# Attention and expert kernel on one core: one PSUM tile throughout, early expert blocks spread over the last pairs, gathers issued ahead of stores, pair 1's input turns placed between pair 0's scores

## The chip, the cores and the metric

The kernel runs on one core of a Trainium2 chip. The core has four engines that work side by side, each through its own instructions in order: TensorE (PE in the profile; its weight loads are shown apart as PEld), VectorE (DVE), ScalarE (ACT) and GpSimd (POOL). SyncE (SP) issues most DMAs; POOL issues the indirect ones (gathers and scatters by a list of row numbers). PE writes its results into PSUM, which has eight banks of 128 partitions by 512 floats; DVE and ACT read them from there ("evacuate" them) into SBUF, the working memory. POOL does not touch PSUM in this kernel. Engines wait for one another by semaphores.

The metric is the time of one execution on the device in microseconds, as the median of several runs. The profile is of one more execution.

## The reference

```python
def _attn_ref(q, k, v):                      # q, k, v: 8 x 8 x 576 x 64
    scores = scale * np.matmul(q, k.transpose(0, 1, 3, 2))
    mask = block_i >= block_j                # causal by blocks of 64
    scores = np.where(mask, scores, -1000000000.0)
    scores = scores - np.max(scores, axis=-1, keepdims=True)
    attn = np.exp(scores)
    attn = attn / (np.sum(attn, axis=-1, keepdims=True) + 1e-09)
    return np.matmul(attn, v)

def _moe_ref(x, w_gate, w1, w2, capacity):   # x: 8 x 576 x 512, capacity 128
    scores = np.einsum('bsd,d->bs', x, w_gate)
    out = x.copy()
    for b in range(B):
        top_idx = np.argpartition(-scores[b], capacity)[:capacity]
        xe = x[b, top_idx]
        h = np.maximum(xe @ w1, 0.0)         # 512 -> 1024
        ye = h @ w2                          # 1024 -> 512
        g = 1.0 / (1.0 + np.exp(-scores[b, top_idx]))
        out[b, top_idx] = x[b, top_idx] + g[:, None] * ye
```

`x` is the attention's output with its heads side by side. So all rows are written once, and the 128 best rows of each batch are read back, sent through the expert and written again.

## The kernel before, in words

**Attention** runs over 32 pairs of heads (4 for each of 8 batches). For a pair p the steps are: `load` and `load_v` (DMAs on SP); `turn_in` (ten transposes on PE for k, ten for q, which write two PSUM banks) and `keep_in` (two evacuations each, on ACT); `scores` (44 matmuls, in three parts called 2, 1 and 0, into the five score areas of `SETS`); `maxima` (nine row maxima on DVE) and `exps` (nine exponentials on ACT that also sum up); `turn_p` and `keep_p` (transposes of the exponentials on PE and their evacuations on ACT and DVE); `times_v` (the product with v); `denom` (on POOL), `keep_x` (DVE), `turn_x` (PE), `invert` and `divide` (DVE). The last pair of a batch also stores the batch's rows and starts `select`.

The order of instructions on every engine is a list written out by hand: `STEPS` gives each step a due time in units of a pair, the plan holds each step at p + its due time, and the loop emits the first step of the sorted plan that may run (`ready`). Five pairs are thus in flight. `BANK` says which of the eight banks a step takes; `take` and `give` keep account of it. In the kernel before, every pair's `turn_in` takes banks 6 and 7, which are also those of the pair's largest score area (`('s', 0)`).

**Selection.** For each batch `select` makes a chain of small steps: `score` (dot products with `w_gate` on DVE, lines 547 to 552), `flip`, `store` and `fetch` through DRAM or `spread` through PE (lines 575 to 585), `tied` and `once` (ties), `below` (five comparisons of all scores with all, on POOL, for the last batch on DVE), `rank` (six matmuls with ones on PE), `spot` and `find` (DVE, lines 622 to 645), after which the batch's row numbers lie in `idx_all`. Ticks in the plan fit these steps in between attention's; what is left over at the end of attention goes to the expert phase. There `compared` is what remains of batch 5, `older` of batch 6, `last` of batch 7.

**Expert phase.** Batches 0 to 3 are group 0, batches 4 to 7 group 1, 128 rows of each. `gather` (line 890) reads the rows back by an indirect DMA on POOL. `turn_parts` (line 901) transposes them: four PE transposes, a high half on ACT and a low half on DVE, since each operand is split in two numbers that are multiplied as three products. `hidden_parts` (line 934) makes one of eight blocks of the hidden layer for a whole group: 12 matmuls of 512 columns, a Relu on ACT (line 944) and the low half on DVE (line 945). `final` (line 954) makes one batch's output: 24 matmuls, with `between()` called in their middle, which turns the next group's rows, and one DVE instruction for y (line 966), whose buffers number two. `store` (line 970) writes the rows back by an indirect DMA on POOL. All indirect DMAs read or write `out_dram`, so a gather and a store wait for one another's landing.

`halves`, `split1` and `split2` make the two numbers of each weight. For `split2` of even blocks ACT makes the high half and DVE the low one; for odd blocks POOL makes both (lines 865 and 866).

Some expert work stands among the last pairs: the plan goes on for pairs 32 to 36, which do not exist, and `stand_in` uses their turns for the transposes of group 0 (`warm`, four of them) and their scores for three hidden blocks (`fill`, three of them). The kernel before lets one absent pair take as many blocks as there are free single-bank areas. Attention's PSUM tile `ps_all` belongs to a pool that ends with attention; the expert phase opens a second pool, `psum2`, over the same banks.

## Time and profile before

| | |
|---|---|
| median of 3 runs | 426.69 us (426.08 to 426.8) |
| profiled execution | 425.77 us, of which 424.1 us is the span from the first to the last instruction |
| mean granted clock of TensorE | 0.976 |
| busy: PE, PEld, DVE, ACT, POOL | 383.7, 276.1, 312.6, 281.0, 225.5 us |
| DMA | 50.35 MB, 119 GB/s over the span |

Busy times are shares of the whole span, but the stages differ: up to about 290 us attention runs, then its last pairs with early expert work, then the expert phase. So the views by stage, the chain of waits and the order of time say more than the sums. A matmul's end is modelled, so a busy PE is not PE at its peak. The granted clock is the share of TensorE's clock that was passed on.

### The profile page before, as it was taken

The page shows a single profiled execution, that of the slowest core. Times are in us where ns is not written, and L with a number is a line of the kernel's source. Part 1 is how long each engine was busy: PE and PEld are TensorE (multiplying, and loading weights), DVE is VectorE, ACT ScalarE, POOL GpSimd, SP SyncE. Part 2 cuts the span into 40 slices and gives each one's busy share as a digit, 9 for nine tenths or more (in the row PEclk, how much of TensorE's full clock was granted, in tenths as well). Part 3 has the DMA queues.
Part 4 walks back from the last instruction along what each step waited for, and adds up shares of the span by engine and source line. Part 5 has one row for each costly group of instructions (what it writes and reads, how often), then busy time and mean ns, then how long its engine had stood idle before and what let it go on. Part 6 is the DMA issues. An engine that isn't in the chain of part 4 may idle for free.

```text
span 424.1 us, 14177 instructions
## 1 busy us (share of the span) xinstructions
PE 383.7 (90%) x5482; PEld 276.1 (65%) x5482; DVE 312.6 (74%) x704; ACT 281.0 (66%) x969; POOL 225.5 (53%) x370
## 2 busy tenths in 40 slices
PE   3779999999999999998999999998979988299995
PEld 2455677667765777666776667765747866288883
DVE  2457778997998899999899999989459983422222
ACT  3679999999999999989999989987213210112100
POOL 2110174337885223997974993897939893200022
PEclk9889999999999999999999999999998999599999
DMA  9745554945887958387558647425003101200011
GB/s 174 168 107 138 135 127 112 244 99 104 231 189 185 262 128 188 78 238 169 121 160 178 152 146 164 103 59 175 2 0 114 49 0 48 78 25 0 2 49 49
DMA packets 128368, 50.35 MB, mean 119 GB/s; under 512 B 119695, under 2 KB 119725, under 8 KB 128301
## 3 DMA queue, kind: packets, MB, share of 16 engines
q1 hardware_dynamic: 125836, 44.96, 43.7%
q0 software_dynamic: 1280, 4.20, 3.1%
q8 instruction: 43, 0.70, 0.7%
q10 hardware_dynamic: 1184, 0.30, 0.3%
q14 instruction: 25, 0.20, 0.2%
HBM read 37.88 MB, written 11.55 MB: 117 GB/s over the span
## 4 chain that ended last, share of the span: by engine, by line
PE 43%; DVE 15%; ACT 14%; POOL 9%; issue 5%; DMA 3%; SPq 1%; POOLq 0%; ACTq 0%; DVEq 0%
ACT p_sb L414 13%; PE h_ps L938 8%; PE ps L455 6%; PE ps L395 6%; PE y_ps L961 6%; PE ps L486 5%; PE ps L335 5%; DVE nmax L404 4%; POOL more L608 3%; PE ps L938 2%; DMA xe<-out_dram,idx_all 2%; POOL rinv L515 2%; DVE pt L228 2%; PE ps L494 1%; POOL beats1a L610 1%
## 5 line engine op out<-in xcount | busy, mean ns | idle before, releaser
L414 ACT ACTIVATE p_sb<-ps,nmax 128x192 f32<-128x192 f32 (+8 forms) x288 | 147.2, 538 | 22.2 <-DVE nmax L404 17.3
L404 DVE TENSOR_REDUCE nmax<-ps 128x1 f32<-128x192 f32 (+8 forms) x288 | 118.9, 476 | 15.3 <-PE ps L395 13.3
L395 PE MATMUL ps<-kT,qT 64*64 64x64 f32 (+6 forms) x1408 | 90.9, 400 | 0.5 <-DVE xeTl L912 0.5
L515 POOL TENSOR_SCALAR rinv<-sum 64x4 f32<-64x4 f32 (+2 forms) x192 | 50.1, 261 | 71.3 <-ACT pt L221 38.5
L486 PE MATMUL ps<-pt,v 128*64 128x256 f32 (+3 forms) x512 | 76.0, 439 | 1.0 <-ACT pt L221 1.0
L486 PEld LDWEIGHTS ps<-pt,v 128*64 128x64 f32 x512 | 33.9, 136 | 60.2 <-issue 54.4
L455 PE MATMUL ps<-ident,p_sb 64*128 64x64 f32 x1472 | 65.6, 227 | 1.9 <-ACT p_sb L414 0.9
L221 ACT COPY pt<-ps 128x256 f32<-128x256 f32 (+2 forms) x160 | 61.3, 429 | 2.5 <-PE ps L455 1.7
L414 ACT ACTIVATION_READ_ACCUMULATOR p_sb<-ps,nmax 128x1 f32 x288 | 62.6, 217 | 0.0
L455 PEld LDWEIGHTS ps<-ident,p_sb 64*128 64x128 f32 x1472 | 55.5, 141 | 7.5 <-issue 2.5
L395 PEld LDWEIGHTS ps<-kT,qT 64*64 64x64 f32 x1408 | 51.2, 139 | 13.6 <-issue 6.6
L228 DVE COPY pt<-ps 128x512 f32<-128x512 f32 (+1 forms) x96 | 50.3, 552 | 9.3 <-PE ps L455 5.3
L961 PE MATMUL y_ps<-w,h 128*128 128x512 f32 x192 | 47.2, 403 | 1.0 <-DVE h L945 1.0
L961 PEld LDWEIGHTS y_ps<-w,h 128*128 128x128 f32 x192 | 36.9, 194 | 9.7 <-DVE h L945 1.4
L608 POOL TENSOR_SCALAR more<-sB,sc 64x576 bf16<-64x576 f32 (+4 forms) x35 | 41.0, 1180 | 0.8
L971 POOL DMA_INDIRECT out_dram<-y,idx_all x8 | 8.4, 1051 | 54.6 <-DVE y L966 46.0
L225 POOL TENSOR_SCALAR vz<-v 64x512 f32<-64x512 f32 x32 | 21.0, 657 | 29.3 <-DMA v<-in_v_dram 23.3
L228 DVE COPY xt<-ps 128x576 f32<-128x576 f32 x32 | 24.2, 756 | 16.5 <-PE ps L494 13.3
L938 PE MATMUL h_ps<-xeTh,w 128*128 128x512 f32 x104 | 34.6, 408 | 0.0
L549 DVE CUSTOM_DVE_ANT_0 junk<-x_sb,wg_b 128x512 bf16<-128x512 f32 x40 | 33.5, 837 | 0.2
L528 DVE TENSOR_TENSOR x_sb<-ps,rinv 128x640 f32<-128x640 f32 x32 | 26.4, 825 | 8.3 <-PE ps L335 8.1
L927 ACT ACTIVATE gate<-gate 128x1 f32<-128x1 f32 x8 | 1.6, 203 | 43.1 <-DVE gate L923 43.1
(99 smaller groups left out, 522.9 us busy)
## 6 DMA issues: line engine op xcount, KB each, us to landing
v<-in_v_dram SPq DMA_DIRECT2D x64, 128.0 KB, 3.2
out_dram<-x_sb SPq DMA_DIRECT2D x8, 1024.0 KB, 5.4
ld_q<-in_q_dram SPq DMA_DIRECT2D x32, 160.0 KB, 3.4
ld_k<-in_k_dram SPq DMA_DIRECT2D x31, 160.0 KB, 4.1
ld_q<-in_q_dram SPq DMA_DIRECT2D x32, 128.0 KB, 4.1
w_raw<-in_moe_w_dram SPq DMA_DIRECT2D x16, 256.0 KB, 3.9
ld_k<-in_k_dram SPq DMA_DIRECT2D x31, 128.0 KB, 4.3
vz<-in_v_dram SPq DMA_DIRECT2D x64, 32.0 KB, 2.9
```

Source lines behind the costliest of these rows:

```text
L221: nc.scalar.copy(out=o, in_=i)
L228: nc.vector.tensor_copy(out=o, in_=i)
L395: nc.tensor.matmul(place(p, t)[64 * o:64 * o + 64, c0:c1], s["qT"][r, tokens(t, hh)], s["kT"][r, tokens(k0 // 64, hh, c1 - c0)], start=Tru ...
L404: nc.vector.tensor_reduce(out=s["nmax"][:, c:c + 1], in_=place(p, t), axis=AX.X, op=ALU.max, negate=True)
L414: nc.scalar.activation(out=st[p]["p"][:, first(t):first(t) + ends(t)], in_=place(p, t), func=AF.Exp, bias=st[p]["nmax"][:, c:c + 1], scale ...
L455: nc.tensor.transpose(out=ps[:, a, at], in_=win, identity=ident[r, r])
L486: nc.tensor.matmul(x[64 * hh:64 * hh + 64, at + c:1024], vt[:, n, hh, :], s["pt"][:, pt_row(hh, n):pt_row(hh, n) + 512 - 128 * n], start=( ...
L515: nc.gpsimd.tensor_scalar(out=r[to:to + 64, hh, i:i + n], in0=s[64 * a:64 * a + 64, c:c + n], scalar1=1e-9, scalar2=None, op0=ALU.add,)
L549: nc.vector.tensor_tensor_reduce(out=junk[:, 0:DM], in0=x[:, t, :], in1=wg_b, scale=1.0, scalar=0.0, op0=ALU.mult, op1=ALU.add, accum_out= ...
L608: eng.tensor_scalar(out=o[r, c:c1], in0=row["sB"][r, c:c1], scalar1=sc[r, t:t + 1], scalar2=None, op0=op)
L938: nc.tensor.matmul(ps[:, 0:ncol], w1_hl[f][:, a, c, :], xeT[g][d][:, c, 0:ncol], start=(c == 0 and t == 0), stop=(c == NC1 - 1 and t == 2),)
L961: nc.tensor.matmul(ps[0:n, 0:DM], h_tile(f)[:, a, begin[g][gi]:begin[g][gi] + n], late["w2"][f][:, d, :], start=(f == 0 and t == 0), stop= ...
```

## The change

- `ps_all` is made once for the whole kernel. In the expert phase `open_bank` hands out its banks in turn: 0 to 3 for tag `w`, 4 and 5 for `s`, 6 and 7 for `wide`. `banks["free"]` goes.
- `SECOND` gives pair 1 its own due times: its k turn right behind pair 0's scores 2, its q turn right behind pair 0's scores 0, its own scores 2 earlier. The inputs of pairs 1 and 2 take banks 2 and 3 (`bank`).
- Matmuls of constants: 11 of 512 columns first of all on PE (`wake(WARM)`), and 4 of 128 columns behind each of pair 0's two input turns.
- An absent pair takes at most one hidden block (`filled`), and one more is emitted right behind the last pair's product with v; its evacuation comes after attention's last step.
- In `split2` ACT makes the high halves of all blocks; POOL makes the low half of the odd ones.
- In the expert phase, batch 5's `once` comes first of all, its rank and its spots each one block later, the weight splits ahead of each hidden block. Batch 6's rank, spots and index come in the middle of the third final tile. The stores of group 0 come behind its fourth tile, and y has four buffers.

```diff
+WARM, WAKE = 11, 4
+SECOND = {
+    ('turn_in', 'k'): 1.1192,
+    ('turn_in', 'q'): 1.3146,
...
+    ('scores', 2): 1.9619,
+}
...
+    psum = ctx.enter_context(tc.tile_pool(name="psum", bufs=1, space=PSUM))
+    ps_all = psum.tile([P, 8, 512], F32, name="ps")
...
+        def bank(p, use):
+            return BANK["x"] if p in (1, 2) and use[0] == "in" else BANK[use]
...
-                    plan.append((p + at, i, p, name, args))
+                    plan.append((SECOND.get((name, *args), p + at) if p == 1 else p + at, i, p, name, args))
...
+        def wake(n, cols=4):
+            for _ in range(n):
+                nc.tensor.matmul(spare()[:, 0:cols * P], ones_b, ones_b.unsqueeze(1).to_broadcast([P, cols, P]), start=True, stop=True)
+        wake(WARM)
...
-                    elif name == "scores" and fill and not warm and len(BANK[use]) == 1 and not any(v for u, v in parts.items() if u[0] == "in"):
+                    elif name == "scores" and fill and p not in filled and not warm and len(BANK[use]) == 1 and not any(v for u, v in parts.items() if u[0] == "in"):
+                        filled.add(p)
...
+                if name == "turn_in" and p == 0:
+                    wake(WAKE, 1)
+                if name == "times_v" and p == N - 1 and fill and not warm:
+                    parts["last"] = list(hidden_parts(0, fill.pop(0), spare()))
...
     def split2(f):
         w = late["w2"][f]
-        halves(late["raw"][:, f, :], w[:, 0], w[:, 1], f % 2 == 1)
+        raw = late["raw"][:, f, :]
+        nc.scalar.copy(out=w[:, 0], in_=raw)
+        eng = nc.gpsimd if f % 2 else nc.vector
+        eng.tensor_tensor(out=w[:, 1], in0=raw, in1=w[:, 0].bitcast(F32), op=ALU.subtract)
...
-        y = late["pool"].tile([P, DM], F32, name="y", bufs=2)
+        y = late["pool"].tile([P, DM], F32, name="y", bufs=4)
...
-        psum = ctx.enter_context(tc.tile_pool(name="psum2", bufs=3, space=PSUM))
-        banks["wide"] = lambda name: psum.tile([P, 2, 512], F32, tag="wide", bufs=1, name=name)
+        turns_of = {"w": [0, 1, 2, 3], "s": [4, 5]}
+        def open_bank(tag, name):
+            x = turns_of[tag].pop(0)
+            turns_of[tag].append(x)
+            return ps_all[:, x, :]
+        banks["wide"] = lambda name: ps_all[:, 6:8, :]
...
         for i, f in enumerate(fill + list(range(EARLY, NC2))):
-            hidden(0, f)
+            if i == 0:
+                run(compared, "tied")
             for _ in range(3):
                 if rest:
                     split2(rest.pop(0))
-            if i == 0:
-                run(compared, "tied", "rank")
+            hidden(0, f)
             if i == 1:
+                run(compared, "rank")
+                run(last, "spread")
+            if i == 2:
                 run(compared, "spot", "find")
                 gather_ready(1)
-                run(last, "spread")
-            if i == 2:
                 run(older, "tied", "below")
                 run(last, "tied")
...
-                stores.append(final(g, gi, lambda: turns(nx if gi == n - 1 else 2)))
+                def between():
+                    if gi == 2:
+                        run(older, "rank", "spot", "find")
+                    turns(nx if gi == n - 1 else 2)
+                stores.append(final(g, gi, between))
...
                 if gi == 1:
                     run(last, "spot", "find")
-                    run(older, "rank")
-                if gi == 2:
-                    run(older, "spot", "find")
                 gather_ready(g + 1)
-                if gi or n == 1:
+                if gi == n - 1 or not nx:
                     for store in stores:
                         store()
                     stores = []
```

More of the change, by code (lines that the diff above doesn't have):

```diff
@@ L124 @@
 PRELOAD = {"load": 3, "load_v": 2}
+WARM, WAKE = 11, 4
+SECOND = {
+    ('turn_in', 'k'): 1.1192,
+    ('turn_in', 'q'): 1.3146,
+    ('keep_in', 'k', 0): 1.1782,
+    ('keep_in', 'k', 1): 1.1802,
+    ('keep_in', 'q', 0): 1.5108,
+    ('keep_in', 'q', 1): 1.5128,
+    ('scores', 2): 1.9619,
+}
 ENGINE = {
@@ L236, in attention @@
         sm = att.enter_context(tc.tile_pool(name="sm", bufs=2))
-        psum = att.enter_context(tc.tile_pool(name="psum", bufs=1, space=PSUM))
-        ps_all = psum.tile([P, 8, 512], F32, name="ps")
         pairs = [(b, h) for b in range(B) for h in range(0, H, 2)]
@@ L245, in attention @@
         live = [None] * 8
+        def bank(p, use):
+            return BANK["x"] if p in (1, 2) and use[0] == "in" else BANK[use]
         def take(p, use, reads):
-            for x in BANK[use]:
+            for x in bank(p, use):
                 assert live[x] is None, (p, use, live)
                 live[x] = [p, use, reads]
-            x = BANK[use]
+            x = bank(p, use)
             return ps_all[:, x[0]:x[-1] + 1, :]
         def give(p, use):
-            for x in BANK[use]:
+            for x in bank(p, use):
                 assert live[x][0:2] == [p, use], (p, use, live)
@@ L286, in attention @@
         banks["hold"] = lambda z: (take(z, "rk", 1)[:, 0, :], lambda: give(z, "rk"))
-        banks["free"] = lambda: any(live[x] is None and room(x) > 0.14 for x in range(8))
         def held(n, shape, name, zero, value=0.0):
@@ L764, in ready @@
                 live[x] is None
-                for use in uses.get(name, lambda *x: [])(*args) if firsts[use] == (name, args) for x in BANK[use]
+                for use in uses.get(name, lambda *x: [])(*args) if firsts[use] == (name, args) for x in bank(p, use)
             )
-        parts = {}
+        parts, filled = {}, set()
         def stand_in(p, name, args):
@@ L861, in load_w2 @@
         del w2_rows[:n]
-    def halves(raw, hi, lo, pool_engine=False):
-        if pool_engine:
-            nc.gpsimd.tensor_scalar(out=hi, in0=raw, scalar1=1.0, scalar2=1.0, op0=ALU.mult, op1=ALU.mult)
-            nc.gpsimd.tensor_tensor(out=lo, in0=raw, in1=hi.bitcast(F32), op=ALU.subtract)
-        else:
-            nc.scalar.copy(out=hi, in_=raw)
-            nc.vector.tensor_tensor(out=lo, in0=raw, in1=hi.bitcast(F32), op=ALU.subtract)
     def split1(f):
         w = w1_hl[f]
-        halves(w1_raw[:, :, f * P:(f + 1) * P], w[:, 0], w[:, 1], True)
+        raw = w1_raw[:, :, f * P:(f + 1) * P]
+        nc.gpsimd.tensor_scalar(out=w[:, 0], in0=raw, scalar1=1.0, scalar2=1.0, op0=ALU.mult, op1=ALU.mult)
+        nc.gpsimd.tensor_tensor(out=w[:, 1], in0=raw, in1=w[:, 0].bitcast(F32), op=ALU.subtract)
     def split2(f):
         w = late["w2"][f]
-        halves(late["raw"][:, f, :], w[:, 0], w[:, 1], f % 2 == 1)
+        raw = late["raw"][:, f, :]
+        nc.scalar.copy(out=w[:, 0], in_=raw)
+        eng = nc.gpsimd if f % 2 else nc.vector
+        eng.tensor_tensor(out=w[:, 1], in0=raw, in1=w[:, 0].bitcast(F32), op=ALU.subtract)
     def run(chain, *names, n=None):
@@ L985, in experts @@
     def experts():
-        psum = ctx.enter_context(tc.tile_pool(name="psum2", bufs=3, space=PSUM))
-        banks["wide"] = lambda name: psum.tile([P, 2, 512], F32, tag="wide", bufs=1, name=name)
-        banks["free"] = lambda: True
-        banks["hold"] = lambda z: (banks["open"]("w", "rk_ps"), lambda: None)
-        banks["open"] = lambda tag, name: psum.tile([P, 512], F32, tag=tag, bufs={"w": 4, "s": 2}[tag], name=name)
+        turns_of = {"w": [0, 1, 2, 3], "s": [4, 5]}
[4 more added lines that the diff above has]
+        banks["wide"] = lambda name: ps_all[:, 6:8, :]
+        banks["hold"] = lambda z: (open_bank("w", "rk_ps"), lambda: None)
+        banks["open"] = open_bank
         open_late()
```

## The prediction, made before the changed kernel ran

> **What bounds the kernel now.** I read the page first, then busy time and granted clock by stage, then the chain that ended last, then the order of time at the places where TensorE (PE) stands idle. The page says that no engine but PE is near its span:
>
> ```profile
> span 424.1 us, 14177 instructions
> PE 383.7 (90%) x5482; PEld 276.1 (65%) x5482; DVE 312.6 (74%) x704; ACT 281.0 (66%) x969; POOL 225.5 (53%) x370
> ```
>
> The 10% are not spread evenly. Stretches of my choice, in us (the first five lie between changes of the clock); the columns are the length, the busy time of PE, PEld, DVE, ACT and POOL, PE's granted clock, DMA share and GB/s:
>
> ```profile
> 14.42:17.83 3.41, 0.37 (x6) 0.11 (x4) 1.89 (x3) 2.69 (x11) 0.00 (x0) 1.00 0.98 199
> 17.83:21.24 3.41, 3.41 (x52) 3.19 (x56) 1.29 (x2) 2.03 (x6) 1.97 (x7) 0.50 0.57 126
> 21.24:24.66 3.42, 2.42 (x38) 1.08 (x30) 3.01 (x8) 2.23 (x11) 0.00 (x0) 1.00 0.55 147
> 24.66:28.07 3.41, 1.56 (x43) 1.46 (x45) 0.95 (x4) 3.41 (x13) 0.70 (x3) 1.00 0.01 2
> 28.07:31.48 3.41, 3.41 (x49) 3.01 (x53) 1.50 (x3) 2.47 (x9) 0.69 (x3) 0.50 0.80 176
> 47.40:50.20 2.80, 2.80 (x52) 1.60 (x49) 2.41 (x8) 2.43 (x10) 1.59 (x6) 1.00 0.63 139
> 304.00:318.10 14.10, 11.03 (x88) 7.72 (x86) 6.37 (x15) 2.00 (x4) 7.03 (x12) 1.00 0.01 1
> 318.10:343.00 24.90, 23.81 (x117) 18.64 (x117) 23.94 (x35) 6.44 (x13) 22.89 (x17) 0.93 0.22 70
> 360.47:368.25 7.78, 0.00 (x0) 0.03 (x1) 3.44 (x10) 0.20 (x1) 1.97 (x2) 0.64 0.21 73
> 368.25:374.07 5.82, 5.82 (x21) 4.98 (x21) 1.38 (x2) 1.17 (x2) 0.98 (x1) 0.61 0.12 45
> ```
>
> Three places lose time: the fill of the pipeline (to about 32 us, clock 0.50 twice), the end of attention (3.1 us idle in 304 to 318, then a stage in which DVE is busy 23.94 of 24.90 us), and 7.78 us without a matmul at 360. Between 40 and 290 us nothing is edited. The chain that ended last shows what the end of the kernel waits for (start, length, what):
>
> ```profile
> 302.00 8.62 PE ps L938 x36
> ...
> 344.60 5.54 PE y_ps L961 x24
> ...
> 353.03 5.04 DMA xe<-out_dram,idx_all
> 358.34 2.75 DMA out_dram<-y,idx_all
> 361.21 0.75 DVE y L966
> 361.96 0.86 DVE here L629 x2
> 362.84 0.76 DVE junk L638
> 364.89 3.22 DMA xe<-out_dram,idx_all
> 368.25 1.94 PE xe_ps L909 x8
> 370.19 4.04 PE y_ps L961 x12
> 374.23 22.48 PE h_ps L938 x96
> ```
>
> A gather of batch 7 (353.03), a store (358.34), the index of batch 6 and its gather (364.89) stand in a row in front of the turns at 368.25.
>
> **Part 1, the start.** In order of time (start, length, engine and line; in brackets the idle time before it and what ended it):
>
> ```profile
> 5.75 0.80 PE L335 MATMUL ps<-ident,ld_k 64*128 64x64 f32 x10 [5.75 <-DMA ld_k<-in_k_dram]
> 9.64 5.05 PE L395 MATMUL ps<-kT,qT 64*64 64x64 f32 x44
> 12.24 0.42 ACT L414 ACTIVATE p_sb<-ps,nmax 128x192 f32<-128x192 f32 x1 [1.82 <-DVE nmax L404]
> 17.73 0.75 PE L335 MATMUL ps<-ident,ld_q 64*128 64x64 f32 x10 [3.04 <-ACT p_sb L414]
> 19.61 1.29 DVE L228 COPY pt<-ps 128x512 f32<-128x512 f32 x2 [2.88 <-PE ps L455]
> 22.43 0.42 ACT L414 ACTIVATE p_sb<-ps,nmax 128x192 f32<-128x192 f32 x1 [1.54 <-DVE nmax L404]
> 32.02 0.42 ACT L414 ACTIVATE p_sb<-ps,nmax 128x192 f32<-128x192 f32 x1 [1.48 <-DVE nmax L404]
> 40.78 0.42 ACT L414 ACTIVATE p_sb<-ps,nmax 128x192 f32<-128x192 f32 x1 [0.38 <-DVE nmax L404]
> 47.47 2.71 PE L395 MATMUL ps<-kT,qT 64*64 64x64 f32 x44
> 49.38 0.42 ACT L414 ACTIVATE p_sb<-ps,nmax 128x192 f32<-128x192 f32 x1 [0.37 <-POOL vz L225]
> ```
>
> The first exponentials of pairs 0, 1, 2, 3 and 4 start at 12.24, 22.43, 32.02, 40.78 and 49.38: distances 10.19, 9.59, 8.76 and 8.60, the last being the steady one. Pair 1 is late because its q turn (17.73) needs banks 6 and 7, which pair 0 holds until its exponentials of them are done (PE idle 3.04, ended by ACT). The change gives it banks 2 and 3 and places both turns and the first scores of pair 1 ahead of that. If every distance becomes 8.60, 1.59 + 0.99 + 0.16 = 2.74 us are gained. The first exponentials also come earlier: pair 0's scores are slow (5.05 against 2.71 later), and the distance from scores to exponentials is 2.60 against 1.91 (47.47 to 49.38), so a warm clock gives 0.69; pair 1's k turn no longer lies ahead of these scores, ten transposes at 0.75 (row 17.73), of which I count 0.7, since its two evacuations stay on ACT ahead of the exponentials. Together 4.1. One pair is likely to meet a cold clock still, half of 0.69 off: **3.8 us**. The bounds: if the clock gains nothing and DVE's copies at 19.61 to 20.90, which stay ahead of pair 1's maxima, hold it, at most 22.43 - 20.90 = 1.5 us and perhaps 0.5 is left; above, 4.8 if pair 1 follows pair 0 faster than 8.60, while no older pair competes for ACT.
>
> The 11 warming matmuls have no row. A 512-column matmul goes by in 5.54 / 24 = 0.23 us (344.60); eleven take 2.5 us, or 5.1 at half the clock, and PE waits 5.75 us for its first data: nothing, or up to 0.4 us where they start late. The 4 small ones behind each of pair 0's turns lie in PE's wait for the evacuation: nothing. Pair 2's turns use banks 2 and 3 too, which pair 0's third turn needs next; ACT's evacuation lies between them already: nothing, or 0.75 (ten transposes) if it comes late. Loads keep their order on SP; a load of pair 4 waits for pair 1's turns, which come earlier. Everything after shifts as a whole, for the order is fixed.
>
> Of the clock, the rows say: a stretch with 0.37 of 3.41 us busy and one with 1.56 of 3.41 were each followed by clock 0.50; one with 2.42 of 3.42 was not. [...] I follow the rows; it widens the range upwards.
>
> **Part 2, early blocks and the shared PSUM tile.** The first row is that of line 549 alone between 318 and 325 us, with the shortest, middle and longest of five; the others are of the order of time:
>
> ```profile
> L549 DVE CUSTOM_DVE_ANT_0 junk<-x_sb,wg_b x5: 692/974/1778, 318.1 to 323.3; 128x512 bf16<-128x512 f32 x5
> ...
> 317.22 0.82 DVE L528 TENSOR_TENSOR x_sb<-ps,rinv 128x640 f32<-128x640 f32 x1
> 318.14 1.11 POOL L865 TENSOR_SCALAR w<-w_raw 128x512 fp32r<-128x512 f32 x1 [6.47 <-DVE x_sb L528]
> 318.19 0.80 PE L335 MATMUL sb_ps<-ident,sc 64*128 64x64 f32 x10 [1.48 <-DVE x_sb L528]
> 342.28 0.68 DVE L945 SCALAR_TENSOR_TENSOR h<-h_ps,h 128x512 fp32r<-128x512 f32 x1
> 343.01 0.50 PE L961 MATMUL y_ps<-w,h 128*128 128x512 f32 x1 [1.01 <-DVE h L945]
> 350.05 1.28 POOL L610 TENSOR_TENSOR beats0b<-beats0b,more 128x576 bf16<-128x576 bf16 x1
> ```
>
> Before, three early blocks stand in one piece (8.62) ahead of the last pair's product with v; then PE waits in turn for that pair's evacuations and, for the release of the whole old PSUM tile, for the last division (1.48). After, one block stays there, one follows the product, one lies between the last two turns. PE can win its 3.1 us of idle, and 1.7 for the clock of 0.93 over 24.9 us, 4.8 in all. But the stage behind belongs to DVE, and the last matmul of the first final product waits for DVE's h (343.01). DVE can begin earlier by PE's waits ahead of the last turn, 3.1 - 1.48 = 1.6 us, less the low halves of two blocks at 0.68, one now ahead of the last division and one right behind it: 0.3 to 1.0, I take 0.7. The five scores of the last batch then take about 6 us on DVE (the last begins 5.2 behind the first), while PE has two blocks, 5.6 us, before their spread: a new PE wait of about 1 us, off the path as long as DVE sets the end. Four first passes over odd w2 blocks leave POOL for ACT (1.11 each on POOL, 4.4 in all; ACT is busy 6.44 of 24.90 us there). A score on DVE takes between 0.69 and 1.78, the long ones beside POOL's work, so DVE may get 0 to 3 us back; I take 1.4. Sum **2.1 us**. From below -1.0: the indices of batch 5 come one block later on DVE, its gather and POOL's comparisons of batch 6 queue behind them. From above 4.0. POOL's comparisons then end not at 351.33 but about 2 us earlier.
>
> **Part 3, gathers ahead of stores.** By the chain above, from 353.03 to 374.23, batch 6 is picked only after the third y, which waits for its buffer, that is for the first store, which waits for the gather of batch 7. After, four y buffers exist, stores come behind the fourth tile, and batch 6's rank stands in the middle of the third. Let E be the end of the second final product, 344.60 + 5.54 = 350.1 now. PE then does half a tile (2.8), six rank matmuls (about 0.8), two more halves (5.5) and arrives at the turns at E + 9.1. The index: rank done at E + 3.6, then 0.86 + 0.76 and about 0.8 of hand-overs, gather out at E + 6.0, landed 3.22 to 5.04 later: E + 9.2 to 11.0. PE waits 0.1 to 1.9, I take 0.7, since 3.22 is the gather at the same place: turns at E + 9.8, where they were at 368.25 = E + 18.1. Gain 8.3. Without the idle stretch the clock holds: 12 matmuls take 2.8 for 4.04, and the eight turns 1.94 x 0.61 = 1.2: 2.0 less. Sum **10.3 us**, bounds 5.5 (POOL late by 3 us, slow gather) and 11.0. The four stores now run one after the other, 4 x 2.75 = 11 us on POOL's queue, behind 22.5 us of hidden blocks; without that cover the next y would wait for them. `banks["free"]` is read nowhere: nothing.
>
> **Sum.** 3.8 + 2.1 + 10.3 = 16.2. The profiled execution took 425.77 (span and 1.67 around it), so 409.6; the median of the runs, 426.69, lies 0.92 higher: **410.5 us**. Lower bounds together give 5.0, or 421.7; upper ones 19.8, or 406.9.
>
> **Rivals.** (a) POOL or the gather holds PE: rank 6 now sits ahead of half a tile in PE's queue and waits for the chain that ended at 351.33; if DVE and PE come 2.1 us earlier and POOL does not, or the gather is a 5.04, PE waits 2 to 4 us more: about 413. For it: POOL is busy 22.89 of 24.90; against: it loses 4.4 us. (b) The start's gain doesn't arrive, since DVE's copies hold pair 1 or the clock stays cold, so the warming doesn't do what it says: 3.3 less, 413.8. For it: the clock was 0.50 twice after short idle; against: no queue waits there for a load. (c) Slower: one tile for all banks is tracked as a whole, so that PE's next block waits until ACT and DVE have read the last one. Each of 13 hidden blocks would expose about 1.3 us (0.68 on DVE and nearly as much on ACT), 8 final tiles 0.75 each: 17 + 6 = 23, some 433; it decides once 16.2 / 1.3 = 13 blocks expose it. Against: 47.40 to 50.20, where PE is busy 2.80 of 2.80 on this same tile beside DVE's 2.41 and ACT's 2.43.
>
> **How the numbers follow.** Forecast (407 to 413) 0.62, (a) 0.16, (b) 0.13, (a) and (b) together (up to 421) 0.06, (c) and the like 0.02, no change 0.01. Holding 8 in 10 takes 406.5 to 416.0. Faster by over 0.2% (about what a measurement of this kernel can tell) 0.96, within 0.01, slower 0.03.
>
> **What would show it.** Right: exponentials of pair 3 near 37 us; no PE wait for the last division, yet PE waiting for DVE's h near 336; both late gathers ahead of all stores and PE idle under 2 us before the last turns, clock 1.00 there; the hidden blocks of group 1 starting near 358. Wrong: pair 3 at 39 or later, rank 6 waiting for POOL, or PE idle above 3 us at the turns.

## The result, and the profile after

The changed kernel takes 411.9 us (median of four executions, 410.73 to 412.17) against 426.75 for the kernel before beside it: a ratio of 0.9642, 95% interval 0.9611 to 0.9674. The forecast was 410.5. The profiled execution took 411.95 us, 410.2 of it the span. Two executions of the experiments below, one of 539.39 us (e2) and one of 2033.32 us (e6), were disturbed and are left out of their medians.

The busy times of its page, and a stretch of 270 us (columns as in the prediction):

```profile
PE 383.2 (93%) x5501; PEld 271.9 (66%) x5501; DVE 313.1 (76%) x704; ACT 282.4 (69%) x973; POOL 219.6 (54%) x366
...
10.00:280.00 270.00, 257.80 (x4734) 179.01 (x4730) 237.75 (x550) 249.43 (x892) 156.84 (x287) 1.00 0.65 157
```

Between 10 and 280 us the granted clock is full. No engine has much less to do; the span shrank around the same work. To see where, I cut every span at three events: **A** runs from the start to the first exponential of pair 31, **B** to the last division of attention, **C** to the first matmul of group 1's hidden blocks, and **D** is the rest. Before, the two outer events are these (the division, 317.22, stands in the prediction):

```profile
286.34 0.42 ACT L414 ACTIVATE p_sb<-ps,nmax 128x192 f32<-128x192 f32 x1 [0.94 <-DVE nmax L404]
...
374.07 0.40 PE L938 MATMUL h_ps<-xeTh,w 128*128 128x512 f32 x1
```

After, in order of time (the first five exponentials are those of pairs 0 to 4; in brackets the idle time ahead and what ended it):

```profile
10.83 0.44 ACT L428 ACTIVATE p_sb<-ps,nmax 128x192 f32<-128x192 f32 x1
19.00 0.42 ACT L428 ACTIVATE p_sb<-ps,nmax 128x192 f32<-128x192 f32 x1 [0.86 <-DVE nmax L418]
27.20 0.42 ACT L428 ACTIVATE p_sb<-ps,nmax 128x192 f32<-128x192 f32 x1 [0.29 <-PE ps L409]
36.13 0.42 ACT L428 ACTIVATE p_sb<-ps,nmax 128x192 f32<-128x192 f32 x1 [0.79 <-DVE nmax L418]
44.51 0.42 ACT L428 ACTIVATE p_sb<-ps,nmax 128x192 f32<-128x192 f32 x1 [0.34 <-POOL vz L235]
...
281.38 0.42 ACT L428 ACTIVATE p_sb<-ps,nmax 128x192 f32<-128x192 f32 x1 [0.94 <-DVE nmax L418]
...
290.73 4.04 PE L500 MATMUL ps<-pt,v 128*64 128x512 f32 x16 [0.96 <-ACT pt L231]
...
313.04 0.82 DVE L542 TENSOR_TENSOR x_sb<-ps,rinv 128x640 f32<-128x640 f32 x1
...
338.64 0.50 PE L984 MATMUL ps<-w,h 128*128 128x512 f32 x1 [2.38 <-DVE h L968]
...
350.21 1.24 POOL L918 DMA_INDIRECT xe<-out_dram,idx_all  x1 [4.01 <-DVE idx_all L655]
353.27 0.96 POOL L918 DMA_INDIRECT xe<-out_dram,idx_all  x1 [1.82 <-DVE idx_all L655]
...
356.58 1.07 PE L932 MATMUL ps<-ident,xe 128*128 128x128 f32 x8 [0.18 <-DMA xe<-out_dram,idx_all]
...
357.26 1.00 POOL L994 DMA_INDIRECT out_dram<-y,idx_all  x1 [3.04 <-DMA xe<-out_dram,idx_all]
...
360.24 0.40 PE L961 MATMUL ps<-xeTh,w 128*128 128x512 f32 x1
```

So A went from 286.34 to 281.38, B from 30.88 to 31.66, C from 56.85 to 47.20, and D stayed at 50.0. The whole gain of 13.8 us between the two spans lies in A (4.96) and C (9.65); B lost 0.78. Both late gathers now go out ahead of the first store (357.26), and the wait of 7.79 us ahead of the last turns is 0.18.

The busy time by stretches of the changed kernel shows two stretches at half the clock (second and fourth row), each behind one in which PE waited (first and third row). The fifth row is the stage that DVE keeps busy, the last the way to the turns, where the long wait stood before:

```profile
287.87:291.28 3.41, 1.80 (x24) 1.20 (x24) 3.41 (x9) 2.26 (x8) 2.78 (x8) 1.00 0.09 20
291.28:294.69 3.41, 3.41 (x20) 1.65 (x18) 0.70 (x1) 0.00 (x0) 3.23 (x3) 0.50 0.00 0
335.65:339.07 3.42, 1.03 (x5) 0.45 (x4) 3.42 (x6) 0.00 (x0) 3.24 (x4) 1.00 0.00 0
339.07:342.48 3.41, 3.01 (x11) 2.00 (x11) 2.98 (x8) 1.17 (x3) 3.41 (x3) 0.50 0.00 0
...
313.04:338.64 25.60, 22.16 (x107) 16.99 (x108) 25.07 (x37) 8.19 (x16) 17.46 (x14) 1.00 0.20 68
347.32:356.58 9.26, 9.08 (x43) 6.88 (x42) 6.89 (x20) 0.41 (x2) 2.19 (x2) 1.00 0.19 58
```

Between 313 and 339 DVE is busy 25.07 of 25.60 us. The chain that ended last says what it does there (start, length, what):

```profile
333.33 1.18 DVE beats1a L618
334.55 0.69 DVE h L968
335.24 1.94 DVE beats1a L618 x2
...
337.98 0.60 DVE h L968
...
341.15 6.17 PE ps L984 x24
...
353.27 3.17 DMA xe<-out_dram,idx_all
```

PE's last matmul of the first final product needs the h made at 337.98, and that one stands in DVE's queue behind comparisons of batch 7 which nobody needs yet.

### The profile page after: what moved, and what is told of

Read it like the earlier page. It is cut to its first block, busy times and chain, and to the rows that moved or that the text cites. A ratio compares the mean times of both kernels' runs of the same rounds, so it can differ in the third digit from the quotient of the medians.

```text
span 410.2 us, 14213 instructions
## 1 busy us (share of the span) xinstructions
PE 383.2 (93%) x5501; PEld 271.9 (66%) x5501; DVE 313.1 (76%) x704; ACT 282.4 (69%) x973; POOL 219.6 (54%) x366
## 4 chain that ended last, share of the span: by engine, by line
PE 43%; ACT 17%; DVE 14%; POOL 10%; issue 5%; DMA 1%; POOLq 0%; SPq 0%; ACTq 0%; DVEq 0%
ACT p_sb L428 15%; PE ps L961 8%; PE ps L469 7%; PE ps L984 6%; PE ps L409 6%; PE ps L500 6%; PE ps L349 6%; POOL more L622 3%; DVE nmax L418 3%; POOL rinv L529 2%; DVE junk L563 2%; DVE pt L238 2%; PE ps L508 2%; POOL beats1a L624 1%; DVE junk L652 1%
## 5 line engine op out<-in xcount | busy, mean ns | idle before, releaser
L409 PE MATMUL ps<-kT,qT 64*64 64x64 f32 (+6 forms) x1408 | 88.8, 387 | 1.2 <-ACT qT L233 0.5
L500 PE MATMUL ps<-pt,v 128*64 128x256 f32 (+3 forms) x512 | 77.6, 446 | 1.0 <-ACT pt L231 1.0
L409 PEld LDWEIGHTS ps<-kT,qT 64*64 64x64 f32 x1408 | 49.2, 133 | 14.5 <-issue 5.7
L984 PE MATMUL ps<-w,h 128*128 128x512 f32 x192 | 46.8, 400 | 2.4 <-DVE h L968 2.4
L984 PEld LDWEIGHTS ps<-w,h 128*128 128x128 f32 x192 | 36.4, 191 | 11.2 <-DVE h L968 3.2
L961 PE MATMUL ps<-xeTh,w 128*128 128x512 f32 x128 | 41.8, 400 | 0.7 <-DVE h L968 0.7
L967 ACT ACTIVATE h<-ps 128x512 fp32r<-128x512 f32 x16 | 9.5, 598 | 38.6 <-PE ps L961 38.6
L563 DVE CUSTOM_DVE_ANT_0 junk<-x_sb,wg_b 128x512 bf16<-128x512 f32 x40 | 33.6, 839 | 0.1
```

The source lines that it names most:

```text
L409: nc.tensor.matmul(place(p, t)[64 * o:64 * o + 64, c0:c1], s["qT"][r, tokens(t, hh)], s["kT"][r, tokens(k0 // 64, hh, c1 - c0)], start=Tru ...
L500: nc.tensor.matmul(x[64 * hh:64 * hh + 64, at + c:1024], vt[:, n, hh, :], s["pt"][:, pt_row(hh, n):pt_row(hh, n) + 512 - 128 * n], start=( ...
L563: nc.vector.tensor_tensor_reduce(out=junk[:, 0:DM], in0=x[:, t, :], in1=wg_b, scale=1.0, scalar=0.0, op0=ALU.mult, op1=ALU.add, accum_out= ...
L961: nc.tensor.matmul(ps[:, 0:ncol], w1_hl[f][:, a, c, :], xeT[g][d][:, c, 0:ncol], start=(c == 0 and t == 0), stop=(c == NC1 - 1 and t == 2),)
L984: nc.tensor.matmul(ps[0:n, 0:DM], h_tile(f)[:, a, begin[g][gi]:begin[g][gi] + n], late["w2"][f][:, d, :], start=(f == 0 and t == 0), stop= ...
```

## The experiments

Every edit is against the changed kernel unless another is named. A, B and C are of each kernel's profiled execution.

| kernel | median us | ratio to before (95%) | A | B | C |
|---|---|---|---|---|---|
| before | 426.75 | | 286.34 | 30.88 | 56.85 |
| changed | 411.9 | 0.9642 (0.9611 to 0.9674) | 281.38 | 31.66 | 47.20 |
| e1: no constant products | 414.43 | 0.9728 (0.968 to 0.9776) | 287.56 | 29.98 | 46.98 |
| e2: pair 1 as before | 414.44 | 0.9737 (0.9675 to 0.98) | 283.90 | 31.67 | 47.16 |
| e3: before, gathers first | 415.31 | 0.9763 (0.9708 to 0.9817) | 284.53 | 30.88 | 47.05 |
| e4: early blocks in one piece | 413.74 | 0.9717 (0.9669 to 0.9764) | 281.33 | 30.88 | 48.17 |
| e5: own PSUM pool for experts | 415.1 | 0.9751 (0.9695 to 0.9807) | 283.36 | 29.98 | 49.58 |
| e6: odd high halves on POOL | 412.56 | 0.969 (0.9638 to 0.9742) | 284.68 | 29.99 | 48.21 |
| e7: low halves first | 409.16 | 0.961 (0.9557 to 0.9663) | 281.59 | 31.64 | 43.83 |
| e8: six more constant products | 411.46 | 0.9641 (0.9592 to 0.9691) | 284.75 | 29.99 | 47.83 |
| e9: old order of the early blocks | 416.29 | 0.9798 (0.9756 to 0.984) | 280.79 | 29.99 | 53.11 |
| e10: e7 with 18 constant products | 410.89 | 0.9623 (0.9565 to 0.9681) | 284.99 | 30.00 | 43.84 |
| e11: e10, a gate later | 409.84 | 0.9596 (0.9537 to 0.9654) | 285.39 | 29.98 | 42.79 |
| e12: e11 without 8 of them | 408.04 | 0.9578 (0.9549 to 0.9606) | 283.82 | 30.00 | 42.76 |

(The kernel before ran again beside each group of experiments, with medians from 425.79 to 426.42. The ratios are to these, and of means, not of medians.)

Read the columns before the medians. B takes only three values: 30.88 where all three early blocks stand in one piece, 29.98 to 30.00 with the change's placing, and 31.64 to 31.67 with the same placing where the clock falls ahead of pair 30's product with v (4.04 us at 290.73 above; the same product of pair 31 takes 2.37). A differs by up to 4 us between kernels that are identical up to there: 280.79 to 284.75 over the changed kernel, e4, e5, e6, e7, e8 and e9, 282.55 on average. The start of before, in before and e3, gave 286.34 and 284.53, 285.44 on average.

What differs between those seven is the clock. A is 280.79 to 281.59 in the four profiles that have one stretch of 3.41 us at half the clock in the start, or none (changed, e4, e7, e9), 283.36 in the one with two (e5), and 284.68 and 284.75 in the two with three (e6, e8). These are e8's three, the last two side by side:

```profile
17.31:20.72 3.41, 3.41 (x30) 1.85 (x24) 2.92 (x8) 1.98 (x8) 1.27 (x4) 0.50 1.15 231
24.13:30.96 6.83, 6.07 (x80) 5.04 (x84) 2.59 (x7) 5.04 (x18) 2.00 (x7) 0.50 0.61 146
```

C lies between 46.98 and 47.83 in the changed kernel, e1, e2 and e8, whose code is the same in that stage.

### Undoing one part at a time

**e1**, no constant products:

```diff
-WARM, WAKE = 11, 4
+WARM, WAKE = 0, 0
```

> The changed kernel without its 11 + 8 matmuls of constants. Theory (of the 5.0 us that the start gained, 28 to 49 us, most comes from where pair 1's turns stand and 1 to 2 us from the clock): pair 0's first exponentials near 11.5 to 12 us instead of 10.8, granted clock 0.50 in at least one stretch before 32 us, pair 4's first exponentials at 45.5 to 46.5 instead of 44.5, total 412.9 to 413.9 us. Rival (the warm clock is most of the start's gain): pair 4 at 48 or later, total 415 us or more. Rival (the constants do nothing, PE waits for data there): 411.9 us.

2.5 us slower by the medians, between the theory and the rival. What the products do stands in the last 24 matmuls of pair 0's scores, in e1 and in the changed kernel:

```profile
11.31 3.69 PE L409 MATMUL ps<-kT,qT 64*64 64x448 f32 x24
```

```profile
10.09 1.95 PE L409 MATMUL ps<-kT,qT 64*64 64x448 f32 x24
```

Without the products they take nearly twice as long and end 2.96 us later, at 15.00 for 12.04. In the three profiles without products (before, e1, e3) pair 0's first exponentials start between 12.05 and 12.24 us, in the eleven with them between 10.43 and 11.17. So the products act on the time of the first scores, by my estimate through the clock: 1.9 times as long is near what half the clock cost at the end (4.04 us for pair 30's product with v, 2.37 for pair 31's). No row of the granted clock shows it: for before it reads 1.00 between 9.64 and 14.42, where pair 0's scores take 5.05 us. Nor do the products make sure of the clock behind the first scores: this profile, the slowest execution of e1 (416.23), has 10.2 us at half the clock in the start, but so has e8, which has the products. Pair 4's first exponentials, at 50.67, are on the rival's side (48 or later), but at 48.23 so are e8's. B and C are no worse.

**e2**, pair 1 in its old order and old banks:

```diff
-SECOND = {
-    ('turn_in', 'k'): 1.1192,
...
-}
+SECOND = {}
...
-            return BANK["x"] if p in (1, 2) and use[0] == "in" else BANK[use]
+            return BANK[use]
```

> The changed kernel with pair 1's due times and banks as before, the constants kept. Theory: pair 1's q turn waits again for pair 0's exponentials in banks 6 and 7; exponentials of pairs 0, 1 and 2 about 10 us apart instead of 8.2; pair 4's first exponentials at 47 to 48 us, total 414.5 to 415.5 us. Rival (the warm clock alone gives the gain): 411.9 to 412.9 us.

2.5 us slower by the medians; the two intervals only just part (from 0.9675 here, up to 0.9674 for the changed kernel). In the profile all of it is in A (B and C are the changed kernel's to 0.04), but 283.90 lies among the values that the changed start gave, 280.79 to 284.75, so the profile alone shows nothing. Nor does it show the step of the theory:

```profile
15.24 0.53 PE L341 MATMUL ps<-ident,ld_q 64*128 64x64 f32 x10 [3.19 <-ACT p_sb L420]
...
19.48 0.42 ACT L420 ACTIVATE p_sb<-ps,nmax 128x192 f32<-128x192 f32 x1 [1.52 <-DVE nmax L410]
```

Pair 1's q turn does wait 3.19 us for pair 0's exponentials, as before. Yet its first exponentials come 8.31 us behind pair 0's (11.17), not 10, and pair 4's at 46.85, hardly later than e5's 46.71 with the new order. The medians say that the order of pair 1 is worth something; how stays open.

**e3**, the kernel before with the third part alone (four y buffers, batch 6's rank and index in the third tile, stores behind the fourth):

```diff
-        y = late["pool"].tile([P, DM], F32, name="y", bufs=2)
+        y = late["pool"].tile([P, DM], F32, name="y", bufs=4)
...
+                    if gi == 2:
+                        run(older, "rank", "spot", "find")
...
-                if gi or n == 1:
+                if gi == n - 1 or not nx:
```

> The kernel before with part 3 alone: batch 6's rank, spots and index in the middle of the third final tile, stores of group 0 behind the fourth, four y buffers. Theory: PE's 7.8 us without a matmul shrink to under 2 us and the cold clock behind them goes: 10.3 to 11 us less than before, 415.7 to 416.4 us. Rival (POOL, which still makes the high halves here, holds the rank of batch 6 and with it PE): a gain of 6 to 8 us, 418.5 to 420.5 us, with PE waiting for beats0b at the rank.

With this part alone the time falls by 11.1 us (from 426.42, the median of the kernel before beside it), of the 14.9 of the whole change; this is the theory. Between the profiles the span falls by 11.6: 9.8 in C, from 56.85 to 47.05, and 1.8 in A, whose code is that of before, so that this is scatter. PE's wait ahead of the turns is gone here too:

```profile
358.79 1.06 PE L909 MATMUL xe_ps<-ident,xe 128*128 128x128 f32 x8 [0.23 <-DMA xe<-out_dram,idx_all]
```

With part 3 alone C is 47.05; with everything it is 47.20. **Part 2 as a whole does nothing in C.**

**e4**, the three early blocks in one piece again:

```diff
-                    elif name == "scores" and fill and p not in filled and not warm and ...
+                    elif name == "scores" and fill and not warm and ...
...
-                if name == "times_v" and p == N - 1 and fill and not warm:
-                    parts["last"] = list(hidden_parts(0, fill.pop(0), spare()))
```

> The changed kernel with the three early blocks in one piece again ahead of the last pair's product with v, one PSUM tile kept. Theory (the spread blocks free the last pair's evacuations, but DVE sets the end of the stage): DVE begins the scores of batch 7 about 0.5 to 1.5 us later, total 412.4 to 413.4 us. Rival (PE sets the stage, two blocks of 2.9 us moved behind the product are won in full): 414.5 us or more. Rival (it is worth nothing or costs): 411.9 us or less.

1.8 us slower by the medians, between the theory and the rival; the intervals overlap a little. B is 30.88, which is 0.9 worse than the change's placing at the full clock, and C is 48.17, 0.3 to 1.2 worse than the 46.98 to 47.83 above. The changed kernel's own profile gained nothing from the placing in B only because its clock fell there.

**e5**, a PSUM pool for the experts alone:

```diff
-    psum = ctx.enter_context(tc.tile_pool(name="psum", bufs=1, space=PSUM))
-    ps_all = psum.tile([P, 8, 512], F32, name="ps")
...
+        psum = att.enter_context(tc.tile_pool(name="psum", bufs=1, space=PSUM))
+        ps_all = psum.tile([P, 8, 512], F32, name="ps")
...
-        banks["open"] = open_bank
+        psum = ctx.enter_context(tc.tile_pool(name="psum2", bufs=3, space=PSUM))
...
+        banks["open"] = lambda tag, name: psum.tile([P, 512], F32, tag=tag, bufs={"w": 4, "s": 2}[tag], name=name)
```

> The changed kernel with a PSUM pool of its own for the experts, as before, so that the first product of the experts' stage waits for the last division of attention. Theory: DVE sets the end of this stage and PE's wait (1.48 us before) lies beside it: 411.9 to 412.9. Rival: PE's wait is paid in full, with the cold clock that an idle PE meets: 413.5 to 415.

3.2 us slower, C 2.4 longer: the rival. In order of time, and the clock behind it:

```profile
314.91 0.79 PE L348 MATMUL sb_ps<-ident,sc 64*128 64x64 f32 x10 [2.70 <-DVE h L967]
```

```profile
314.65:318.06 3.41, 3.15 (x16) 2.58 (x17) 3.27 (x10) 2.27 (x5) 0.41 (x1) 0.50 0.90 319
```

PE waits 2.70 us for DVE's h, which reads the old tile, and behind that the clock falls. That DVE is busy all the time did not make PE's wait free.

**e6**, the first pass over odd w2 blocks back on POOL:

```diff
-        nc.scalar.copy(out=w[:, 0], in_=raw)
+        if f % 2:
+            nc.gpsimd.tensor_scalar(out=w[:, 0], in0=raw, scalar1=1.0, scalar2=1.0, op0=ALU.mult, op1=ALU.mult)
+        else:
+            nc.scalar.copy(out=w[:, 0], in_=raw)
```

> The changed kernel with the first pass over odd w2 blocks (128x512, 1.11 us each, four of them) back on POOL. Theory: POOL's passes make DVE's scores long (0.69 to 1.78 us) and DVE sets the end of the stage: 0.5 to 1.5 us slower, 412.4 to 413.4. Rival: POOL has slack there and DVE's scores are long either way: 411.4 to 412.2; or POOL's comparisons of batch 6 end 4.4 us later and PE waits for them: 414 or more.

0.7 us slower by the medians, within the scatter; C is 48.21, 0.4 to 1.2 longer than the 46.98 to 47.83 above. The reason I gave for it is half right. The groups by line with their shapes (count, busy us, mean ns) give DVE's five scores of batch 7 (L549 or L563), before, after and in e6, and the low halves that DVE makes:

```profile
L549 DVE CUSTOM_DVE_ANT_0 junk<-x_sb,wg_b 128x512 bf16<-128x512 f32 x5 | 6.1, 1213 | 0.2
```

```profile
L563 DVE CUSTOM_DVE_ANT_0 junk<-x_sb,wg_b 128x512 bf16<-128x512 f32 x5 | 6.3, 1263 | 0.1
...
L900 DVE TENSOR_TENSOR w<-w_raw,w 128x512 fp32r<-128x512 f32 x4 | 3.1, 806 | 0.0
```

```profile
L563 DVE CUSTOM_DVE_ANT_0 junk<-x_sb,wg_b 128x512 bf16<-128x512 f32 x5 | 6.0, 1199 | 0.1
...
L903 DVE TENSOR_TENSOR w<-w_raw,w 128x512 fp32r<-128x512 f32 x4 | 4.6, 1176 | 0.0
```

The scores cost about the same three times. What e6 lengthens is DVE's own low halves, from 3.1 to 4.6 us. POOL's passes do make the scores long, though, in each of these kernels, and the low halves in the same way. Three rows of the changed kernel show how:

```profile
314.38 0.68 DVE L563 CUSTOM_DVE_ANT_0 junk<-x_sb,wg_b 128x512 bf16<-128x512 f32 x1
...
314.72 1.49 POOL L900 TENSOR_TENSOR w<-w_raw,w 128x512 fp32r<-128x512 f32 x1 [6.32 <-ACT w L898]
...
315.11 1.65 DVE L563 CUSTOM_DVE_ANT_0 junk<-x_sb,wg_b 128x512 bf16<-128x512 f32 x1
```

The score that starts ahead of POOL's pass takes 0.68 us. The next one starts inside the pass and ends 0.55 us behind its end (316.21). All fourteen profiles agree: of these scores and low halves between 310 and 345 us, the 58 that start inside one of POOL's passes over a weight end 0.53 to 0.55 us behind that pass, and the 61 that start while POOL is idle take 0.67 to 0.69 us. In the changed kernel three of the five scores and one of DVE's four low halves start inside such a pass; in e6, where POOL has more passes, all five scores, some of them near the pass's end, and three of the low halves.

**e9**, the old order in the loop over the early blocks:

```diff
         for i, f in enumerate(fill + list(range(EARLY, NC2))):
-            if i == 0:
-                run(compared, "tied")
+            hidden(0, f)
             for _ in range(3):
                 if rest:
                     split2(rest.pop(0))
-            hidden(0, f)
+            if i == 0:
+                run(compared, "tied", "rank")
...
```

> The changed kernel with the order of steps in the loop over the three early blocks as before (hidden block ahead of the comparisons of batch 6, rank 6 and spread 7 where they stood), all else changed. Theory: PE waited 1.06 us for the score of batch 7 (320.94) and 2.38 for h (338.64) in the changed kernel, DVE sets the end of this stage, so the order of PE's work does nothing: 411.5 to 412.5. Rival: the new order costs time, since rank 6's index is later on DVE: 409.5 to 411; or it is what hides spread 7: 413 to 414.5.

(The rank in question is batch 5's; the expectation names batch 6 by mistake. The lines left out move batch 5's rank and index ahead by one block, as before.) 4.4 us slower, C 5.9 longer, more than either of the rivals allowed: my theory that this order does nothing fell. In order of time on PE, ACT and POOL:

```profile
318.71 0.28 PE L633 MATMUL ps<-ties,ones_b 128*128 128x288 bf16 x1 [4.78 <-POOL ties L609]
...
313.77 0.60 ACT L967 ACTIVATE h<-ps 128x512 fp32r<-128x512 f32 x1 [2.80 <-PE ps L961]
314.26 1.65 ACT L898 CAST w<-w_raw 128x512 fp32r<-128x512 f32 x3
...
315.47 1.39 POOL L900 TENSOR_TENSOR w<-w_raw,w 128x512 fp32r<-128x512 f32 x1 [8.84 <-ACT w L898]
316.82 1.84 POOL L609 TENSOR_TENSOR ties<-ties,later 128x640 bf16<-128x640 bf16 x1
```

The ties of batch 5 stand on POOL behind the low half of an odd block. That low half now waits 8.84 us for ACT's high half, and ACT makes it (314.26) only behind the Relu of a block (313.77). PE waits 4.78 us at the third matmul of the rank. Moving the high halves to ACT makes POOL's queue hang on ACT's; pulling `tied` to the front of the loop is what pays for it. In e3 the old order stands with POOL making both halves, and C is 47.05. The two edits of part 2 that I costed apart are one.

### What the wait for h costs, and a better version

**e7**, the second half of batch 7's comparisons behind the three blocks, its rank in the middle of the second tile:

```diff
-            if i > 1:
-                run(last, "below", n=2)
+        run(last, "below")
...
+                    if gi == 1:
+                        run(last, "rank")
...
-                    run(last, "spread", "tied", "below", "rank")
+                    run(last, "spread", "tied", "below")
```

> The changed kernel with the order of DVE's work at the end of attention changed: the second comparisons (below) of batch 7 come behind all three early expert blocks instead of two by two between them, so that DVE makes the low halves of f6 and f7 first, and rank 7 is issued in the middle of the second final product. Theory: in the changed kernel PE waits 2.38 us for DVE's h ahead of the last matmul of the first final product (338.64) and runs cold behind it (339.07 to 342.48); with h ready early neither is left, some 2.4 + 0.6 = 3 us, so 408.5 to 409.5 against 411.9. Rival: DVE's work is only moved; rank 7 and then POOL's comparisons of batch 6 come later, PE waits at rank 6 or at the turns: 410.5 to 412.5.

2.7 us faster than the changed kernel by the medians, as the theory had it, though the intervals of the two ratios overlap. C is 3.4 shorter, 43.83 here and 43.84 in e10, which has the same code there. Both low halves are made at once, and the first final product runs through, at the full clock:

```profile
331.23 1.28 DVE L968 SCALAR_TENSOR_TENSOR h<-ps,h 128x512 fp32r<-128x512 f32 x2
...
333.43 5.77 PE L984 MATMUL ps<-w,h 128*128 128x512 f32 x24
...
353.40 1.07 PE L932 MATMUL ps<-ident,xe 128*128 128x128 f32 x8 [1.22 <-DMA xe<-out_dram,idx_all]
```

**e8**, constant products in two more of PE's waits at the end of attention:

```diff
+                if name == "times_v" and p == N - 2:
+                    wake(4)
...
+                if name == "turn_in" and p == N + 1 and args[0] == "k":
+                    wake(2)
```

> The changed kernel with six more warming matmuls (128x512, 0.23 us each at the full clock): four ahead of the product with v of pair 30 (PE was idle 0.96 us there) and two ahead of the stand-in turns behind the last pair (idle 0.65 us). Theory: the clock of 0.50 from 291.28 to 294.69 of the changed kernel goes away and 1.7 us with it; the one behind the wait for h (339.07) stays, so the last division is 30.0 us behind the first exponentials of pair 31 instead of 31.7, and the time is 409.5 to 411.5. Rival: the stage behind takes the gain back, since POOL's comparisons of batch 6 set rank 6 and DVE sets h: 411.5 to 412.5; or the warming matmuls delay the product: 412.5 to 413.

B is 29.99 and the time 411.46 against 411.9, too little to tell. In the four profiles with these products (e8, e10 to e12) the clock never falls in B; in the seven with the same placing and without them it falls in three (changed, e2, e7) and not in four (e1, e5, e6, e9). That the clock loss in B costs 1.68 us is shown; that the products prevent it is not.

**e10** is e7 with e8's six products and twelve more ahead of the first four `turn_p`:

```diff
-        parts, filled = {}, set()
+        parts, filled, idle_turns = {}, set(), [4, 3, 2, 3]
...
+                if name == "turn_p" and idle_turns:
+                    wake(idle_turns.pop(0))
```

> The kernel that makes the low halves first, with the six warming matmuls of the end and twelve more in the waits of PE in front of the first four turns of probabilities (4, 3, 2 and 3; PE was idle 1.94, 1.06, 0.73 and 0.95 us there). Theory: the clock stays full from the first scores on, which saves one or two stretches of 3.41 us at half the clock in the start, up to 1.7 us each, and the one near 291: 406 to 408, against 409.2 for low halves first alone. Rival: the matmuls stand in front of the turns and scores by more than PE's idle time and the clock falls all the same: 409 to 411.

1.7 us slower than e7 by the medians, with overlapping intervals, and on the rival's side. Between the two profiles A is 3.4 longer and B, where e7's clock fell, 1.6 shorter. The first two batches, in order of time:

```profile
14.42 1.04 PE L756 MATMUL ps<-ones_b 128*128 128x512 bf16 x4
...
21.90 0.81 PE L756 MATMUL ps<-ones_b 128*128 128x512 bf16 x3 [1.97 <-ACT p_sb L428]
```

A constant product needs a bank. The first batch found one free; the next two waited for ACT to have read theirs (1.97 and 0.95 us), with all of PE's queue behind them, and pair 2 began at 30.69 (27.20 in the changed kernel).

**e11** is e10 with the third tile's gate on DVE behind batch 6's index:

```diff
                     if gi == 2:
                         run(older, "rank", "spot", "find")
+                        gate(g, gi)
...
-                if gi + 1 < n:
+                if gi + 1 < n and gi != 1:
```

> The same with the gate of the third tile behind the index of batch 6 on DVE (the gate is 0.68 us of a reduction and a chain of 0.5 us around ACT, and stood ahead of that index at 346.52 to 347.66). Theory: the last gather goes out 1.1 us earlier and PE's wait of 1.22 us ahead of the last turns shrinks to 0.1: 1 us under the run without it, 405 to 407. Rival: the gather of batch 7, still on its way, holds POOL's queue, so that the last one lands no earlier: the same as the run without it.

1.05 us under e10 both in the median and in C: the theory's difference, though not its time, which counted from a faster e10. The intervals overlap; C is 42.79 here and 42.76 in e12. The last gather goes out earlier and PE's wait for it is gone:

```profile
354.50 1.06 PE L938 MATMUL ps<-ident,xe 128*128 128x128 f32 x8 [0.24 <-DMA xe<-out_dram,idx_all]
```

**e12** keeps only the first batch of the twelve:

```diff
-        parts, filled, idle_turns = {}, set(), [4, 3, 2, 3]
+        parts, filled, idle_turns = {}, set(), [4]
```

> Low halves first, the gate of the third tile later, six warming matmuls at the end of attention, and of the twelve in the start only the first four, ahead of the first turn of probabilities. Theory: in the run with all twelve, the second, third and fourth batch waited for their bank (1.97 us for an exponential of ACT where PE had been idle 1.06 before, then 0.95) and put pair 2 back by 3 us; the first batch cost nothing. Without them the start is that of the changed kernel (first exponentials of pair 2 near 27 to 29 us), and the time is 405 to 407.5. Rival: the clock falls in the start as often as the matmuls saved, so pair 2 is no earlier and the time stays at 408.5 to 410.

408.04 us, all six executions within 408.0 to 408.66, between the two expectations. The wait for banks is gone, but the clock still falls in the start:

```profile
23.16:29.99 6.83, 6.29 (x82) 5.04 (x84) 2.81 (x8) 4.82 (x17) 2.00 (x7) 0.50 0.64 157
```

Its interval, 0.9549 to 0.9606, lies under the changed kernel's: this version beats both kernels. It is not told apart from e7 (0.9557 to 0.9663).

## Why the prediction was right, and where it was not

**The total.** 16.2 forecast, 14.9 measured by the medians and 13.8 between the two profiles. That it came so near is in part chance: by the profiles part 1 gave 1.2 more than forecast, part 2 3.0 and part 3 0.5 less. The rival that would have been slower did not occur: D, which holds group 1's blocks and tiles, is 50.0 before and after.

**Part 3, 10.3.** Right, by its own steps: 9.8 in C when done alone. E, the end of the second final product, is 341.15 + 6.17 = 347.32 after. PE arrived at the turns at E + 9.1 as worked out (it is busy 9.08 of the 9.26 us from E to 356.58), the last gather went out at E + 5.95 (E + 6.0), took 3.17 (3.22 taken), and PE waited 0.18 where 0.7 was allowed. The clock in that stretch was 1.00, as expected. Rival (a) did not occur: POOL was done in time for the rank.

**Part 1, 3.8.** Pair 0's first exponentials come 1.41 earlier (12.24 to 10.83), where 0.69 + 0.7 was taken. The term for the distances, 2.74, rests on a reading that the runs do not bear out: e3 has the start of before and its wait for banks 6 and 7 (3.04), and pair 1 is 8.31 behind pair 0 there, not 10.19. So that wait alone does not set the first distance; pair 0's slow scores, 5.05 us in before and 3.81 in e3, are part of it. The pair of profiles shows 4.96, and the distances behind pair 0 are 8.17, 8.20, 8.93 and 8.38, mostly under the 8.60 that I took as the steady one; only the upper bound allowed for that. But the average of seven starts against two says 2.9. A single pair of profiles can't give this term to better than a microsecond or two, which the forecast did not know. Pair 3 at 36.13 is where it was looked for (near 37), but with the same start e6 and e8 have it at 39.70 and 39.85, past the 39 that was to show the part wrong. Rival (b) is no separate case: it is what the clock does in some executions (three stretches of 3.41 us at 0.50 in the start of e6 and e8, none in that of the changed kernel).

**Part 2, 2.1.** This step failed in size. B and C together are 77.93 with part 3 alone (e3); with part 2 they are 78.86 in the profile of the changed kernel and 76.96 in that of e1, which has the same code there: a loss of 0.9 or a gain of 1.0, inside the bounds (-1.0 to 4.0) but under the value taken. Two of its terms are why. The 1.4 for DVE's scores never came: they cost 6.1 us before and 6.3 after. POOL lost its first passes, but its low halves still lie under the scores, and three of the five still wait one out (the rows under e6). And the clock, which I let only widen the range, is a term: half a clock from 291.28 to 294.69 costs 1.68 in B, and the same from 339.07 follows PE's wait for h. The 0.7 for DVE's earlier beginning holds where the clock does: 0.9 in B.

The reading behind the part was half right. DVE does set the end of this stage, as forecast, and PE waits for its h (2.38 at 338.64, looked for near 336), while the wait for the last division is gone. But "DVE-bound" is not "any wait of PE is free", as e5 shows (2.4), and the stage also hangs on POOL and ACT, as e9 shows (5.9). The cheapest gain was in the order of DVE's queue, which the change leaves alone (e7: 3.4).

Undone one by one, the parts cost 2.5, 2.5, 1.8, 3.2, 0.7 and 4.4, and part 3 alone gains 11.1: together far more than 14.9. The edits cover for one another, so neither their sum nor a single undoing says what one is worth alone. By the medians parts 1 and 2 add 3.4 to part 3, by the ratios 5.2; the intervals do not settle which.

**The clock.** The forecast followed rows of before in which half a clock came behind stretches with PE busy for 0.37 and 1.56 of 3.41 us, and let that only widen the range. The new rows bear the old ones out: the clock was 0.50 behind 287.87 to 291.28, 53% busy, and behind 335.65 to 339.07, 30% busy. The sum would have been nearer with one such stretch taken as a term (16.2 less 1.7 is 14.5).

## What to carry to other kernels

Issue reads that somebody waits for ahead of writes that nobody waits for; that was two thirds of the gain. On an engine that is busy all the time, sort its queue by who waits: two low halves pulled ahead of comparisons gave 3.4 us in that stage. Before you cost edits one by one, ask which of them makes another one's queue wait, and cut the profile at fixed events so that scatter in one stage is not read as the effect of an edit in another. Then compare stages of kernels that share their code: what one profile shows of the start here means little below 4 us.

## What the runs showed of the hardware

Between 10 and 400 us the granted clock of before and of the changed kernel is 1.00 or 0.50, and its changes lie 3.41 us or a multiple of it apart (half the clock for three times 3.41 and once 10.24 us in before, for twice 3.41 in the changed kernel), at other times in each profile. Over the fourteen profiles each stretch of 3.41 us at the full clock, counted from such a change, in which PE was busy for 43% or less was followed by half the clock (11, 21 and 38% in before, 30% in the changed kernel); none with 64% or more was; between 45% and 62% both happened (half the clock behind 46% in before, 51% in e7 and 53% in the changed kernel, the full clock behind 45% in e9, 52% in e7 and 55% in the changed kernel). The same code in B took 29.98 or 31.66 us, and the same start differed by 4 us. What decides between 45% and 62%, and with it whether PE's short waits in B cost 1.7 us, no run shows.

DVE's scores and its low halves of the weights have both inputs in SBUF. Those that started inside one of POOL's passes over 128x512 floats of a weight ended 0.53 to 0.55 us behind the pass in all 58 cases under e6, where 0.67 to 0.69 was their length beside an idle POOL. DVE's low half of h, which has one of its inputs in PSUM, showed nothing of it: the fifteen that start inside such a pass take 0.68 to 0.69 us (0.68 at 323.21 in the changed kernel, inside the pass from 323.15 to 324.44). So what POOL cost DVE here depended on where each instruction started, and not on how long POOL was busy. Why the two kinds differ no run shows.
